# A fused Fourier mixing and SoLU block: sixteen-row exchange of the reciprocals through DRAM, and its two turns at other places

## The chip, the cores and the metric

The kernel runs on one core of one Trainium2 chip. A core has TensorE (PE, with a separate path PEld that loads weights), VectorE (DVE), ScalarE (ACT), GpSimd (POOL) and SyncE (SP), and 16 DMA engines that move data between DRAM and the on-chip memory. Transfers are issued from the instruction queues of SP, ACT and POOL; an issue waits in its queue like any other instruction. The metric is the device time of one execution in microseconds (us), lower is better, as the median of several runs.

## The reference

The first block is a Fourier mixing along the sequence, the second a feed-forward layer whose activation is `h * softmax(h)` followed by a normalization over the 1024 hidden features:

```python
# x: (8, 3136, 256); filt: (1569, 256); w_in: (256, 1024); w_out: (1024, 256)
X = np.fft.rfft(x, axis=1)
y = np.fft.irfft(X * (filt_r + 1j * filt_i)[None], n=3136, axis=1)
h = y.reshape(25088, 256) @ w_in
e = np.exp(h - h.max(-1, keepdims=True))
solu = h * e / (e.sum(-1, keepdims=True) + 1e-09)
mu = solu.mean(-1, keepdims=True)
var = ((solu - mu) ** 2).mean(-1, keepdims=True)
out = ((solu - mu) / np.sqrt(var + 1e-06) * g_ln) @ w_out
```

All data are float32.

## The kernel before

**Work and stages.** The transform of each of the 8 batch elements is done as small matrix products with tables (lines 244 to 424), with passes through DRAM between its parts. Element 0 is transformed ahead of the main loop (up to about 75 us); those of elements 1 to 7 are spread over the main loop, by the steps that `PLAN` gives (line 39), and the last ends at about 1200 us.

The MLP works on 196 blocks of 128 tokens. Two blocks are a pair (98 pairs); both of its matrix products are done on pairs with seven products in place of eight, whose sums and differences POOL makes (`pair_sums`, L782, and `project_sums`, L921). Four blocks are a group g (49 groups). The main loop (L1225) calls `step(k)` for k = 0 to 204; each step writes out by hand what each engine gets and in which order (`manual_schedule`), so that the order of calls in `step` is the order in every queue. A step takes some 6 to 8 us.

**One group on its way.** For block k: PE makes h (`product`, L793, seven products a pair); ACT copies a part out of PSUM (`keep`, L811) and DVE adds the rest and takes the running minimum for the softmax (`finish`, L813: L822 and L825). A `finish` frees a PSUM bank which one of PE's next products needs. Two steps later ACT takes the exponential (L835), DVE multiplies (`normalize`, L847) and a step after that turns the 32x32 squares of the result (`turn`, L865, called the solu turn here). SP then regroups the turned data by eight transfers a pair (`regroup`, L882) into `solu_t`, where hidden features are on partitions; these wait until earlier products have read the buffer. POOL sums them, PE projects them with `w_out` (`project`, L937), ACT scales a part by the reciprocal of the standard deviation (`keep_out`, L968), DVE scales and adds the rest (`finish_out`, L972), and SP stores the output (`store_out`, L980).

**The reciprocals' exchange.** A group's reciprocals come to lie with tokens in an order that differs from the order of the output's rows: POOL computes them for the 128 partitions and four blocks in `deviations` (L890 to L893, by a power of -0.5, into columns 0 to 3 of the 128x32 tile `lines`) in step k = 4g + 6. Then

- in step 4g + 7, after all else that DVE does in that step, `regroup_deviations` (L909) turns `lines` by 32x32 squares on DVE (the first turn, L912), and SP copies rows 0 to 3 of each of the four squares to rows a, a + 32, a + 64 and a + 96 of `corners`, by four transfers of 4 rows of 128 bytes (L914);
- in step 4g + 8, after all else that DVE does, `place_deviations` (L916) turns that half of `corners` on DVE (the second turn, L919). From then on column 2 * (p % 2) + i holds the scale of the i-th output block of pair p.

The first users are `keep_out(p, 0, (0, 0))` on ACT and `finish_out(p, 0, 0, (0, 0), 1)` on DVE in step 4g + 9, for p = 2g. PE's product 6 of that step writes on in the bank that this `keep_out` reads. The 49th group does without the exchange (`product_deviations`, L901).

**What sets the order.** SP's queue holds, in step order: the store of an output pair, the loads of x (four transfers, L270, in some steps), the four transfers of the exchange, eight transfers of `solu_t`, and so on. Every issue waits in order. The framework gives each transfer one of eight completion semaphores in turn, so that an issue also waits for the transfer eight places before it.

Of the kernel before, what the change touches and what calls it, by code (L numbers as in the profile page):

```python
# [9 lines left out]
FP32 = mybir.dt.float32  # L10
# [3 lines left out]
ALU = mybir.AluOpType  # L14
# [4 lines left out]
P = 128  # L19
# [89 lines left out]
def kernel(  # L109
# [10 lines left out]
    nc = tc.nc  # L120
# [12 lines left out]
        name="turn_tbl").ap()  # L133
    one_dram = nc.inline_tensor(np.eye(P, dtype=np.float32), name="one_tbl").ap()

    def pool(name, bufs, space=None, stack=ctx):
        kw = {} if space is None else {"space": space}
        return stack.enter_context(tc.tile_pool(name=name, bufs=bufs, **kw))

    consts = pool("consts", 1)  # L140
    dram = pool("dram", 1, DRAM)
# [2 lines left out]

    d1 = [dram.tile([NS, P, C], FP32, name=f"d1_{e}") for e in range(B)]
    d2 = [dram.tile([NS, P, C], FP32, name=f"d2_{e}") for e in range(B)]
    f_dram = dram.tile([NP, 2, NQ, 2, C], FP32, name="f_dram")

    wf_t = consts.tile([NR, NK], FP32, name="wf_t")
# [9 lines left out]
    neg_half, floor_sb = small_consts[:, 0:4], small_consts[:, 4:5]  # L159
# [278 lines left out]
    with ExitStack() as st:  # L438
# [145 lines left out]
        for i0, n, rows in ((0, 4, P), (4, 4, P), (8, NP - 9, P), (NP - 1, 1, NQ)):  # L584
            f, at = filters[i0]
            nc.sync.dma_start(
                out=f_dram[i0:i0 + n].rearrange("i u q k c -> (u q) i (k c)")[0:rows],
                in_=f[0:rows, at:at + n].rearrange("p i k c -> p i (k c)"))
# [8 lines left out]
        for i in range(pieces):  # L597
# [6 lines left out]
            for j in range(0, 2, size):  # L604
                (nc.scalar.copy, nc.vector.tensor_copy)[j](
                    out=pairs_x[:, 2 * i + j:2 * i + j + size].rearrange("p a c t -> p a t c"),
                               in_=ps[:, j:j + size].rearrange("p a (t c) -> p a t c", t=2))
# [36 lines left out]
        for at, i in enumerate(order):  # L644
# [9 lines left out]
            i0, n = sp.units[i]  # L654
# [42 lines left out]
    lines = small.tile([P, 32], FP32, name="lines", tag="lines", bufs=1)  # L697
    corners = spread.tile([P, 2, 32], FP32, name="corners", tag="corners")
# [59 lines left out]
    def load_de(sp, u, dma=nc.scalar.dma_start):  # L758
# [6 lines left out]
    turns, variances, solu_ts, solu_sums, spreads, rss, pos, ots, places, regrouped = (  # L765
        {} for _ in range(10))
# [93 lines left out]
    def turn(k):  # L860

        g, i = divmod(k, 4)
        if i == 0:
            turns[g] = turn_pools[1 - g % 2].tile([P, DFF // 32, 4, 32], FP32, name=f"turn_{g}", tag="turn")
        nc.vector.transpose(out=turns[g][:, :, i, :],  # L865
                            in_=solus[k].rearrange("p (f j) -> p f j", j=32))
# [23 lines left out]
    def deviations(g):  # L890
        rs = small.tile([P, 4], FP32, name=f"rs_{g}", tag="rs", bufs=2)
        nc.gpsimd.tensor_tensor(out=rs, in0=variances.pop(g), in1=floors.pop(g), op=ALU.add)
        nc.gpsimd.tensor_tensor(out=lines[:, 0:4], in0=rs, in1=neg_half, op=ALU.pow)  # L893

        if 2 * g == pairs - 2:
            spreads[g] = wide = pools["diff"].tile([P, 4, 32], FP32, name=f"wide_{g}", tag="diff")
            nc.gpsimd.tensor_tensor(
                out=wide, in0=turn_t[:, 0:32].rearrange("p (o i) -> p o i", o=1).broadcast_to([P, 4, 32]),
                in1=lines[:, 0:4].rearrange("p (b o) -> p b o", o=1).broadcast_to([P, 4, 32]), op=ALU.mult)

    def product_deviations(g, ps):  # L901

        wide = spreads.pop(g)
        nc.tensor.matmul(out=ps, lhsT=wide.rearrange("p b i -> p (b i)"), rhs=turn_t[:, 32:36],
                         start=True, stop=True)
        rss[g] = corners[:, g % 2, 0:4]
        nc.scalar.copy(out=rss[g], in_=ps)

    def regroup_deviations(g):  # L909

        places = corners[:, g % 2, :]
        nc.vector.transpose(out=lines, in_=lines)  # L912
        for a in range(4):
            nc.sync.dma_start(out=places[a:P:32, :], in_=lines[32 * a:32 * a + 4, :])  # L914

    def place_deviations(g):  # L916

        rss[g] = places = corners[:, g % 2, :]
        nc.vector.transpose(out=places, in_=places)  # L919

    def project_sums(p, step):  # L921
# [44 lines left out]
    def keep_out(p, i, to):  # L966
        rs = out_half(p, i, 0)[1]
        nc.scalar.activation(out=out_half(p, *to)[0], in_=pos[p, 0], func=AFT.Copy, scale=rs)  # L968
# [14 lines left out]
    blocks = NT * B // 2  # L983
# [85 lines left out]
    def step(k):  # L1069
        j, odd = divmod(k, 2)  # L1070
        p = j - (LAG - 1) // 2 if odd else j - (LAG + 1) // 2
        if not 0 <= p < pairs:
            p = None
# [24 lines left out]
        if not odd:  # L1098
# [50 lines left out]
            if 0 <= j - 3 < pairs and j % 2:  # L1149
                deviations((j - 3) // 2)  # L1150
# [13 lines left out]
        else:  # L1164
# [3 lines left out]
                finish(j, k, 1, (k - 1, 1), 2)  # L1168
            for job in early[k]:
                job()  # L1170
            if proj:
                project(p, 1)
                keep_out(p, 0, (0, 0))
                project(p, 2)
                finish_out(p, 0, 0, (0, 0), 1)
# [9 lines left out]
                job()  # L1185
            if 3 <= k < blocks + 3:
                turn(k - 3)
            if hid:
                finish(j, k - 1, 1, None, 0)
                finish(j, k, 0, (k, 0), 2)  # L1190
# [5 lines left out]
                square(k - 3)  # L1196
            for job in first_parts[k]:
                job()
        if k >= 7 and k % 4 == 3 and k - 3 < blocks:
            regroup_deviations((k - 7) // 4)  # L1200
        if k >= 8 and k % 4 == 0 and k - 4 < blocks:
            place_deviations((k - 8) // 4)
        if k < 3:
            convert_w_out(k + 1)
        if k == 2:
# [4 lines left out]
            prepare_w_out(k)  # L1210
        for job in late[k] + loads[k]:
            job()
        if k < 4:
            scale_w_out(k)

# [41 lines left out]
```

## Time and profile before

| what | value |
|---|---|
| time, median of 3 runs | 1580.31 us (1578.24 to 1582.49) |
| time of the profiled execution | 1574.98 us |
| its span, first to last instruction | 1573.1 us |
| granted TensorE clock, mean | 0.996 |
| DVE / ACT / POOL busy share | 80% / 58% / 72% |
| first turn L912 | 48 times, 196 to 209 ns |
| second turn L919 | 48 times, 194 to 214 ns |
| exchange transfers L914 | 192 issues, 0.497 to 1.25 us each on SP, median 0.566 |
| POOL's power L893 | 49 times, 1.02 to 1.37 us |
| mean DMA rate, 160 to 1200 us / 1200 to 1530 us | 211 / 115 GB/s |

The profile is a record of one execution. A line of the timeline gives start and duration in us, the engine, the source line, the operation with the tiles that it writes and reads, how many were merged, and in brackets the engine's idle time before it with what ended it. A line of the waits gives who waited for what, the total in us, how often, and the longest wait. A line of the windows gives the length and then each engine's busy time in the order PE, PEld, DVE, ACT, POOL, the granted clock, the busy share of the DMA engines and the GB/s. The profiled execution was 5.33 us shorter than the median of the runs, so that times of the trace are compared with each other and differences are carried over.

### The profile page before, as it was taken

The page shows a single profiled execution, that of the slowest core. Times are in us where ns is not written, and L with a number is a line of the kernel's source. Part 1 is how long each engine was busy: PE and PEld are TensorE (multiplying, and loading weights), DVE is VectorE, ACT ScalarE, POOL GpSimd, SP SyncE. Part 2 cuts the span into 40 slices and gives each one's busy share as a digit, 9 for nine tenths or more (in the row PEclk, how much of TensorE's full clock was granted, in tenths as well). Part 3 has the DMA queues.
Part 4 walks back from the last instruction along what each step waited for, and adds up shares of the span by engine and source line. Part 5 has one row for each costly group of instructions (what it writes and reads, how often), then busy time and mean ns, then how long its engine had stood idle before and what let it go on. Part 6 is the DMA issues. An engine that isn't in the chain of part 4 may idle for free. (4 is left out here: it accounts for less than half of the span.)

```text
span 1573.1 us, 36938 instructions
## 1 busy us (share of the span) xinstructions
PE 1523.8 (97%) x12748; PEld 1050.9 (67%) x12748; DVE 1254.2 (80%) x2329; ACT 918.6 (58%) x1850; POOL 1135.9 (72%) x1300
## 2 busy tenths in 40 slices
PE   8987999999999999999999999999999999999997
PEld 5633666667666776667666676667766777777776
DVE  5879878897888798977988788877898777777773
ACT  3564655656556656665556656566565665666663
POOL 2577787787768677887768767786766766666675
PEclk9999999999999999999999999999999999999999
DMA  9857787777886788666877588766764554344444
GB/s 246 257 198 211 215 234 219 228 204 206 234 243 199 192 232 249 195 181 185 240 218 197 157 224 234 225 175 181 224 212 124 133 133 122 101 106 116 107 109 115
DMA packets 343795, 298.20 MB, mean 190 GB/s; under 512 B 29451, under 2 KB 313109, under 8 KB 343609
## 3 DMA queue, kind: packets, MB, share of 16 engines
q1 hardware_dynamic: 280408, 175.92, 42.1%
q0 software_dynamic: 29568, 87.33, 18.3%
q10 hardware_dynamic: 33634, 32.58, 7.1%
q8 instruction: 104, 1.70, 0.5%
q14 instruction: 81, 0.66, 0.1%
HBM read 118.02 MB, written 74.84 MB: 123 GB/s over the span
## 5 line engine op out<-in xcount | busy, mean ns | idle before, releaser
L952 PEld LDWEIGHTS o<-w_out_sb,solu_t 128*128 128x128 f32 x3136 | 382.0, 192 | 47.5 <-issue 43.3
L801 PE MATMUL m<-w_in_sb,s 128*128 128x512 f32 x784 | 395.3, 605 | 10.8 <-ACT h L811 5.8
L952 PE MATMUL o<-w_out_sb,solu_t 128*128 128x128 f32 x3136 | 401.0, 276 | 1.8 <-DVE ot L972 1.7
L952 PEld LDWEIGHTS o<-w_out_sb,u 128*128 128x128 f32 x2352 | 306.9, 192 | 141.3 <-issue 107.4
L801 PE MATMUL m<-w_in_sb,y 128*128 128x512 f32 x588 | 307.6, 606 | 10.9 <-DVE nmax L825 8.7
L952 PE MATMUL o<-w_out_sb,u 128*128 128x128 f32 x2352 | 310.4, 275 | 5.2 <-ACT ot L968 3.1
L811 ACT COPY h<-m 128x512 f32<-128x512 f32 x294 | 172.9, 588 | 227.4 <-PE m L801 186.9
L780 POOL TENSOR_TENSOR u<-solu_t 128x512 f32<-128x512 f32 x98 | 138.7, 1415 | 230.7 <-DMA solu_t<-turn 177.1
L847 DVE SCALAR_TENSOR_TENSOR h<-e,h 128x1024 f32<-128x1024 f32 x196 | 296.5, 1513 | 0.4 <-ACT e L835 0.4
L968 ACT ACTIVATE ot<-o,corners 128x128 f32<-128x128 f32 x392 | 143.4, 367 | 254.8 <-PE o L952 240.1
L825 DVE CUSTOM_DVE_ANT_0 h<-m,h 128x512 f32<-128x512 f32 x196 | 134.3, 685 | 162.1 <-ACT h L811 96.6
L855 ACT ACTIVATE h<-h,nmu 128x1024 f32<-128x1024 f32 x196 | 225.0, 1148 | 57.3 <-DVE turn L865 57.2
L865 DVE STREAM_TRANSPOSE turn<-h 128x1024 f32<-128x1024 f32 x196 | 242.3, 1236 | 1.9
L835 ACT ACTIVATE e<-h,nmax 128x1024 f32<-128x1024 f32 x196 | 225.3, 1150 | 4.1 <-DVE h L847 3.4
L780 POOL TENSOR_TENSOR u<-solu_t,u 128x512 f32<-128x512 f32 x98 | 139.5, 1424 | 78.2 <-PE o L952 78.0
L801 PEld LDWEIGHTS m<-w_in_sb,s 128*128 128x128 f32 x784 | 128.0, 191 | 97.3 <-issue 85.0
L780 POOL TENSOR_TENSOR u<-u,solu_t 128x512 f32<-128x512 f32 x98 | 165.7, 1691 | 11.0 <-DMA out_dram<-ot 2.4
L972 DVE SCALAR_TENSOR_TENSOR ot<-o,corners,ot 128x128 f32<-128x128 f32 x299 | 103.5, 347 | 85.4 <-ACT ot L968 53.2
L801 PEld LDWEIGHTS m<-w_in_sb,y 128*128 128x128 f32 x588 | 95.6, 190 | 109.0 <-DVE nmax L825 41.5
L780 POOL TENSOR_TENSOR solu_t<-solu_t,solu_t 128x512 f32<-128x512 f32 x98 | 144.8, 1478 | 0.9
L780 POOL TENSOR_TENSOR s<-y 128x128 f32<-128x128 f32 x196 | 103.0, 526 | 5.2 <-ACT y L423 4.7
L396 PEld LDWEIGHTS py<-wb_t,t 50*64 50x64 f32 x3584 | 57.6, 134 | 42.9 <-issue 20.2
(122 smaller groups left out, 1913.2 us busy)
## 6 DMA issues: line engine op xcount, KB each, us to landing
solu_t<-turn SPq DMA_DIRECT2D x780, 128.0 KB
out_dram<-ot SPq DMA_DIRECT2D x196, 128.0 KB
t<-d POOLq DMA_DIRECT2D x112, 200.0 KB, 6.1
d<-x POOLq DMA_DIRECT2D x100, 200.0 KB, 4.9
t<-d ACTq DMA_DIRECT2D x37, 512.0 KB
f<-f_dram POOLq DMA_DIRECT2D x37, 512.0 KB, 7.5
d<-g POOLq DMA_DIRECT2D x36, 512.0 KB, 4.5
x<-in_x_dram SPq DMA_DIRECT2D x112, 98.0 KB
```

The lines of the kernel that those rows point to most:

```text
L396: nc.tensor.matmul(out=views[g][64 * h:64 * h + 64, cb, i, :], lhsT=t4[rows, i, c0:c0 + 64], rhs=wb_t[rows, 0:N1], start=True, stop=True)
L780: nc.gpsimd.tensor_tensor(out=out, in0=in0, in1=in1, op=op)
L801: nc.tensor.matmul(out=ms[j, bank], lhsT=lhsT, rhs=w_in_sb[:, w, :], start=m in (1, 2, 7), stop=True, skip_group_check=True)
L811: nc.scalar.copy(out=h_half(k, i), in_=ms[j, 0])
L825: nc.vector.tensor_tensor_reduce(out=h_half(k, i), in0=ms[j, bank], in1=h_half(*kept), scale=1.0, scalar=sofar, op0=ALU.add, op1=ALU.min, ...
L835: nc.scalar.activation(out=e, in_=hs[k], func=AFT.Exp, bias=nmaxs.pop(k)[:, 1:2], scale=-1.0, accum_out=esums[g][:, i:i + 1])
L847: nc.vector.scalar_tensor_tensor(out=solu, in0=e, scalar=SHRINK, in1=solu, op0=ALU.mult, op1=ALU.mult, accum_out=nmu)
L855: nc.scalar.activation(out=solu, in_=solu, func=AFT.Square, bias=nmu, scale=-float(DFF), accum_out=variances[g][:, i:i + 1])
L865: nc.vector.transpose(out=turns[g][:, :, i, :], in_=solus[k].rearrange("p (f j) -> p f j", j=32))
L952: nc.tensor.matmul(out=pos[p, bank], lhsT=lhs[:, f, :], rhs=w[:, f, :], start=f == 0 and (m in (1, 2, 7) or alone), stop=True, skip_group_ ...
L968: nc.scalar.activation(out=out_half(p, *to)[0], in_=pos[p, 0], func=AFT.Copy, scale=rs)
L972: nc.vector.scalar_tensor_tensor(out=ot, in0=pos[p, bank], scalar=rs, in1=out_half(p, *kept)[0], op0=ALU.mult, op1=ALU.add)
```

## The change

The first turn of a group follows the solu turn of the same step (4g + 7). One transfer stores the sixteen rows that matter to a tile in DRAM, `exchange`, of which there are two; a second one, issued after the loads of that step, fetches them back in the other order. The second turn stands half a step later: in step 4g + 9, behind the step's first `finish` and the early jobs, ahead of the first projection. So that one access pattern covers the sixteen rows, the reciprocals are in every eighth column (0, 8, 16 and 24) of `lines` and, after the second turn, of `corners`.

```diff
+    exchange = [dram.tile([16, 32], FP32, name=f"exchange_{n}") for n in range(2)]
...
     def deviations(g):
...
-        nc.gpsimd.tensor_tensor(out=lines[:, 0:4], in0=rs, in1=neg_half, op=ALU.pow)
+        nc.gpsimd.tensor_tensor(out=lines[:, 0:32:8], in0=rs, in1=neg_half, op=ALU.pow)
...
     def regroup_deviations(g):
 
+        nc.vector.transpose(out=lines, in_=lines)
+        nc.sync.dma_start(out=exchange[g % 2], in_=lines[0:P:8, :])
+
+    def fetch_deviations(g):
+
+        nc.sync.dma_start(out=corners[0:P:8, g % 2, :],
+                          in_=exchange[g % 2].rearrange("(a b) c -> b a c", b=4))
+
+    def place_deviations(g):
+
         places = corners[:, g % 2, :]
-        nc.vector.transpose(out=lines, in_=lines)
-        for a in range(4):
-            nc.sync.dma_start(out=places[a:P:32, :], in_=lines[32 * a:32 * a + 4, :])
-
-    def place_deviations(g):
-
-        rss[g] = places = corners[:, g % 2, :]
+        rss[g] = places[:, 0:32:8]
         nc.vector.transpose(out=places, in_=places)
...
     def step(k):
...
         else:
             if hid and k >= LAG:
                 product(j, 5)
                 keep(j, k - 1, 1)
                 finish(j, k, 1, (k - 1, 1), 2)
             for job in early[k]:
                 job()
+            if k >= 9 and k % 4 == 1 and k - 5 < blocks:
+                place_deviations((k - 9) // 4)
             if proj:
                 project(p, 1)
                 keep_out(p, 0, (0, 0))
...
             if 3 <= k < blocks + 3:
                 turn(k - 3)
+            if k >= 7 and k % 4 == 3 and k - 3 < blocks:
+                regroup_deviations((k - 7) // 4)
             if hid:
                 finish(j, k - 1, 1, None, 0)
                 finish(j, k, 0, (k, 0), 2)
...
-        if k >= 7 and k % 4 == 3 and k - 3 < blocks:
-            regroup_deviations((k - 7) // 4)
-        if k >= 8 and k % 4 == 0 and k - 4 < blocks:
-            place_deviations((k - 8) // 4)
...
         for job in late[k] + loads[k]:
             job()
+        if k >= 7 and k % 4 == 3 and k - 3 < blocks:
+            fetch_deviations((k - 7) // 4)
```

`product_deviations` takes its columns by the same step of eight. The changed kernel's lines stand one or more further down: the first turn is still L912, the store is L913, the fetch L917, the second turn L924, `keep_out` L973, `finish_out` L977.

## The prediction

> **What bounds the kernel now.** I read, in this order, the page's busy times, the sums by window, the list of waits, and the timeline around the exchange.
>
> ```profile
> PE 1523.8 (97%) x12748; PEld 1050.9 (67%) x12748; DVE 1254.2 (80%) x2329; ACT 918.6 (58%) x1850; POOL 1135.9 (72%) x1300
> ```
> ```profile
> 160.00:1200.00 1040.00, 1024.48 (x9337) 701.17 (x9334) 872.47 (x1603) 621.44 (x1255) 793.55 (x919) 1.00 0.75 211
> 1200.00:1530.00 330.00, 329.69 (x2337) 238.93 (x2336) 243.68 (x486) 203.84 (x412) 225.01 (x247) 1.00 0.44 115
> ```
>
> The first engine column of the windows is PE. While spectra and MLP run together (160 to 1200 us) PE is idle 1040.00 - 1024.48 = 15.5 us; in the tail (1200 to 1530) 0.3 us. So PE sets the time, at a granted clock of 1.00, and nothing that the change touches can win more than those 15.5 us and what the start and the last 45 us hold. The question is how much of the 15.5 us hangs on the exchange.
>
> ```profile
> DVE corners L919 <- DMA corners<-lines: 19.2, 13, 4.1
> ```
> ```profile
> SPq L914 <- DVE lines L912: 133.4, 36, 7.8
> ```
>
> DVE's second turn (L919) waits for the exchange's transfers 13 times, 19.2 us in all, and SP stands 133.4 us in front of the first of them. What a wait of L919 does is seen in group g = 9 (four blocks of tokens; 48 groups use the exchange):
>
> ```profile
> 434.78 5.07 SPq L270 DMA_DIRECT2D x<-in_x_dram  x4
> 439.94 3.91 SPq L914 DMA_DIRECT2D corners<-lines  x4
> ...
> 447.64 0.21 DVE L919 STREAM_TRANSPOSE corners<-corners 128x32 f32<-128x32 f32 x1 [4.08 <-DMA corners<-lines]
> ...
> 448.82 0.68 DVE L825 CUSTOM_DVE_ANT_0 h<-m,h 128x512 f32<-128x512 f32 x1
> ...
> 449.56 1.13 PE L801 MATMUL m<-w_in_sb,y 128*128 128x512 f32 x2 [1.35 <-DVE nmax L825]
> ```
>
> The bracket is the engine's idle time and what ended it. DVE stands 4.08 us at L919; behind it is the next step's `finish` (L825), which frees the bank of product 4; PE stands 1.35 us for that.
>
> **The change, part by part.** Sums are made against the profiled execution, 1574.98 us (span 1573.1 and 1.9 around it). The median of the runs is 1580.31, 5.33 above; I carry the difference over to it.
>
> *Place waits that go.* L919 waits 1 us or more at 187.69 (3.34), 447.64 (4.08), 511.07 (1.00), 637.47 (1.41), 820.64 (1.20), 971.82 (2.31), 1003.73 (1.24), 1035.15 (3.56) and 1061.61 us (1.67). PE idles for `nmax` right behind five of them: at 189.28 (0.34), 449.56 (1.35), 639.00 (0.62), 973.38 (0.84) and 1036.71 (1.14). The gap at 822.30 (1.65) is released by ACT, which had been held by its own DMA issues, and isn't counted. Sum 4.29. In the changed kernel L919 stands behind that `finish`, so even a wait there no longer holds it: **-4.3 us**.
>
> *First turn earlier.* Today L912 follows `normalize`; now it follows the solu turn (L865), 2.4 to 3.9 us earlier in the groups after the first. It needs POOL's power (L893): its end lies at least 0.85 us before the end of that L865 in all 48 groups, so DVE doesn't wait. But its 0.20 us (L912: 48 times, 196 to 209 ns) now stands ahead of L822 and L825, for which PE waits:
>
> ```profile
> 242.06 1.13 PE L801 MATMUL m<-w_in_sb,y 128*128 128x512 f32 x2 [0.62 <-DVE h L822]
> ```
> ```profile
> 1203.29 1.12 PE L801 MATMUL m<-w_in_sb,y 128*128 128x512 f32 x2 [0.32 <-DVE h L822]
> ```
>
> From the end of L822 to PE's next product 1 it is 0.07 us where PE waits (these two), 0.11 to 0.15 in groups 8, 19, 20, 21 and 31, 0.32 or more elsewhere and 1.04 in the tail. So 2 x 0.20 + 5 x 0.13 = **+1.0 us** (ends 0 and 9.6 = 48 x 0.20). Behind `normalize` the same 0.20 goes; no PE gap of the trace ends on the turn that gains it.
>
> *Second turn later.* L919 (0.20 us) leaves the end of the even step and stands in the odd step behind `finish` and ahead of the first `finish_out`. ACT's `keep_out` (L968) needs it. In the quiet group at 722 us `finish` ends at 723.49 and `keep_out` starts at 723.07; so it slips to about 723.75, ends at 724.1, and PE's product 6, which needs it, comes at 725.48. Hidden with 1.4 us to spare; ACT then idles 2.01 us before its next `keep_out`, so its exponential catches up. Cost 0.
>
> *Two legs in place of four transfers.* SP issues two instead of four: 2 x 0.57 us less per group (L914 median 0.566), on an engine that waits 133 us here: 0. But the fetch waits until the store has landed, and behind it on SP stand the eight solu_t transfers (L882) of the next pair, then its two stores of the output. The x loads of the same step lie between the two legs only in the first group. No transfer of 2 KB through DRAM is in the trace. Nearest rows: the present 512-byte transfers, whose packets alone have 128 bytes. In the quiet tail their packets move 1.21 us after the issue and a waiting DVE starts 0.5 to 1.2 us after the last packet (I take 0.65); with queues full the packets come 2 to 5.2 us after the issue. The far end is the 128 KB store of the output, issued at 1542.39 and waited for until 1546.69: 4.3 us. I take the present transfers, for size and queue. Quiet (group 40): L865 ends 1359.07, store issued 1359.50, landed 1361.5, fetch landed 1363.4; L919 is due at about 1369. Full (group 9, where SP is late from L270, so the store still goes at 439.94): 439.94 + 3.58 + 0.65 = 444.17; fetch 444.27 + 3.58 + 0.65 = 448.50. Product 6 without its stall would start at 450.52 - 1.30, and needs the place turn and `keep_out` 0.65 before: 448.57. Just in time. Done so for groups 1 to 46, the fetch misses that point in five (1, 5, 15, 28 and 29, by 0.38, 0.16, 0.84, 0.72 and 1.48: 3.6 us). That is the upper end; the lower is 0, since SP has issued nothing since the store and the fetch finds its own queue empty. I take **+0.5**.
>
> *solu_t.* By the same working its transfers start 0.2 to 3.0 us earlier in 34 of 46 groups, up to 2.0 later in 12. POOL's sums of them end 2.3 us or more before PE reads them in all pairs up to the last three, so this moves PE neither way before the end.
>
> *The end.* There the order on SP does count:
>
> ```profile
> 1535.92 5.66 SPq L882 DMA_DIRECT2D solu_t<-turn  x8
> 1541.68 1.30 SPq L980 DMA_DIRECT2D out_dram<-ot  x2
> ```
> ```profile
> 1546.69 0.37 ACT L968 ACTIVATE ot<-o,corners 128x128 f32<-128x128 f32 x1 [1.78 <-DMA out_dram<-ot]
> ```
> ```profile
> 1547.21 1.13 PE L952 MATMUL o<-w_out_sb,u 128*128 128x128 f32 x8 [1.72 <-ACT ot L968]
> ```
>
> L882 stood directly behind the four corners transfers. Now the store would go at 1531.35 (L865 ends 1530.92), land at 1533.3, and SP is free at about 1533.9, so the store goes 1.9 us earlier and PE's 1.72 us gap can close. But the last pairs' solu_t start at 1543.78, behind a DVE turn that doesn't move, and the gap of 2.02 at 1556.15 waits for sums of them. Between 0 and -1.7 I take **-0.9**.
>
> Sum: -4.3 + 1.0 + 0.5 - 0.9 = -3.7: 1571.3 in the profile's terms, **1576.6** in the runs'.
>
> **The rivals.**
>
> *Given back.* L919 waits 1.0, 1.24 and 1.67 us at 511, 1004 and 1062 us and no PE gap follows: waits are absorbed, and a PE that runs ahead may meet the next late thing. Against it: the gaps after 1204 us are nil, so what is won before is kept. Time 1580.
>
> *More is won.* x loads stand behind solu_t on SP; where it starts earlier, DVE's differences (803.12: idle 1.17 for x, then PE 0.63 at 805.26) and POOL's sums (PE 1.03 at 208.47, and 1.09 at 204.53) could come in time: 2.75 more, with the end's other 0.8 and no late fetch (0.5): -7.7, 1572.6. Against it: in the groups there (2 and 20) solu_t moves by 0.2 and 0.5 us only.
>
> *Slower: DRAM legs late under load.* The point that decides is product 6 of the odd step. With my upper row latencies the slack is -1.48, -0.84, -0.72, -0.38, -0.16, 0.08, 0.26, 0.74 and 0.80 us in the nine tightest. If the two legs together take 1 us more than that, nine groups miss by 10.7 in all: -4.3 + 1.0 + 10.7 - 0.9 = +6.5, 1587. For it: the DMA share is 0.75 in that stretch, and one group's first packet came 5.2 us after its issue. Against it: the emptied queue. The Trainium skill (DMA: Bandwidth & Descriptors, Latency and other measured facts) gives access to HBM, which is the DRAM here, 0.2 us on average and 2 us at high load, and its Specifications add a read-modify-write under 512 B, against rows of 128 B here. No run here shows either yet; if both legs paid 2 us, an estimate by the same slacks is some 38 us slower.
>
> *It doesn't do what it says.* DVE's and SP's listed orders show both turns moved and four transfers made two in each of the 48 groups; PE, ACT and POOL keep their order. Excluded.
>
> **How the numbers follow.** Forecast 0.45 (its own range 1573 to 1580), given back 0.12, more won 0.20, slower 0.23. 0.3% is 4.7 us, about what a measurement of this kernel can tell from no change. Faster than 1575.6: more won, and 0.14 of the forecast: 0.34. Slower than 1585: 0.23. Within: 0.43. The range reaches from 1570 (more won, less 2 us of spread between runs) to 1587, where half of the slower case is left out.
>
> **What would show it.** Right: L919's waits nearly gone, or without a PE gap behind them; the PE gaps at 449 and 1036 us closed; the two gaps behind L822 about 0.2 longer; fetch issued some 2 us after the store in the tail; PE idle between 160 and 1200 us near 12. Wrong: L968 waiting for L919 and PE for L968 in the full groups; SP standing 4 us or more between the legs; POOL waiting longer for solu_t with PE behind it.

## The result, and the profile after

The changed kernel takes 1595.02 us (median of 4 runs, 1591.98 to 1601.16), the kernel before 1579.28 in the same comparison: ratio **1.0104, 95% interval 1.0063 to 1.0144**, slower by some 16 us. The prediction was 1576.6 (1570 to 1587): wrong in sign, and outside the range.

The profiled execution took 1591.98 us (span 1589.9, 16.8 more than before, granted clock 0.992). The busy times, and the windows with the same columns as before:

```profile
PE 1533.9 (96%) x12748; PEld 1054.8 (66%) x12748; DVE 1260.2 (79%) x2329; ACT 919.2 (58%) x1850; POOL 1125.4 (71%) x1300
```
```profile
160.00:1200.00 1040.00, 1016.56 (x9248) 694.12 (x9240) 864.43 (x1578) 611.97 (x1237) 771.84 (x909) 1.00 0.75 208
1200.00:1530.00 330.00, 330.00 (x2348) 237.89 (x2347) 249.14 (x493) 204.84 (x413) 227.43 (x251) 1.00 0.45 117
```

PE idles 23.4 us between 160 and 1200 us (15.5 before) and not at all in the tail. It is also 10.1 us *busier* with as many instructions. Its clock explains some 6.8 of them: it is at 0.50 for 13.7 us more than before, 3.4 of these ahead of 160 us and 10.2 behind (below). The rest isn't explained. I set the start of PE's product 1 of each pair against the same one of before. It is 2.9 us later already at pair 0, ahead of the first exchange; 3.3 at pair 10; 10.6 at pair 15; 13.6 at pair 23 and 13.5 at pair 55; 18.3 at pair 57; 17.3 at pair 61; from pair 72 to the end 16.6 to 17.1. So the time is lost in a few places of the stretch with spectra, and the tail is neutral. The steps at pairs 15, 23 and 57 (5.7, 4.0 and 3.6 us) make 13.2 of the 14.2 us lost between pair 0 and the end; PE's stalls at 331, 463 and 991 us, which are shown below, lie there. The waits of the changed kernel (who, for what, total us, times, longest):

```profile
ACT ot L973 <- DVE corners L924: 42.0, 33, 5.2
...
DVE corners L924 <- DMA corners<-exchange: 16.6, 8, 5.4
DVE diff L280 <- DMA x<-in_x_dram: 15.9, 11, 3.6
...
PE o L957 <- ACT ot L973: 13.3, 8, 4.8
```

The last line is new in size (3.1 before, all of it behind 1530 us): PE waits for `keep_out`, `keep_out` for the second turn, the second turn for the fetch. ACT's 42.0 us alone are no loss: they are as long where no transfer is late (the turns alone, below). DVE's wait for x is 9.4 us before. What PE waits for between 160 and 1200 us, after and before:

```profile
PE o L957 <- ACT ot L973: 11.4, 6, 4.8
PE m L802 <- DVE nmax L826: 5.4, 4, 2.2
```
```profile
PE m L801 <- DVE nmax L825: 6.0, 7, 1.4
PE m L801 <- ACT h L811: 3.7, 3, 1.9
```

There is no wait for `keep_out` in that stretch before. SP's own waits between 160 and 1200 us, first after, then the line of before that answers to it:

```profile
SPq L917 <- DMA exchange<-lines: 146.9, 33, 6.7
...
SPq L883 <- DMA t<-d: 41.6, 14, 7.9
```
```profile
SPq L914 <- DVE lines L912: 76.9, 22, 7.8
```

SP stands 4.5 us on average between store and fetch in each of these 33 groups; in the kernel before it stood for the first turn, in 22 groups and for half as long in all. Group g = 9, the same as in the prediction, over all engines:

```profile
442.04 1.74 SPq L985 DMA_DIRECT2D out_dram<-ot  x2
442.57 0.17 DVE L912 STREAM_TRANSPOSE lines<-lines 128x32 f32<-128x32 f32 x1
...
443.89 2.30 SPq L271 DMA_DIRECT2D x<-in_x_dram  x4
...
446.52 0.53 SPq L913 DMA_DIRECT2D exchange<-lines  x1
...
454.61 0.69 DVE L280 TENSOR_TENSOR diff<-x 113x512 f32<-113x512 f32 x1 [1.58 <-DMA x<-in_x_dram]
454.80 0.57 SPq L917 DMA_DIRECT2D corners<-exchange  x1
455.46 8.33 SPq L883 DMA_DIRECT2D solu_t<-turn  x8
...
456.87 1.02 PE L802 MATMUL m<-w_in_sb,y 128*128 128x512 f32 x2
...
461.90 0.21 DVE L924 STREAM_TRANSPOSE corners<-corners 128x32 f32<-128x32 f32 x1 [5.38 <-DMA corners<-exchange]
462.20 0.37 ACT L973 ACTIVATE ot<-o,corners 128x128 f32<-128x128 f32 x1 [6.41 <-DMA solu_t<-turn]
...
462.71 2.05 PE L957 MATMUL o<-w_out_sb,u 128*128 128x128 f32 x8 [4.82 <-ACT ot L973]
```

The first turn is done at 442.74, but SP is still issuing output stores and x loads, so the store goes 3.8 us later. Its 128-byte packets move for 11 to 13 ns each, the last of them 7.7 us after the issue. The fetch is issued 8.3 us behind the store, its packets come 4.0 to 6.1 us later. From turn to turn it is 19.2 us, and PE stands 4.82. The bracket of `keep_out` names solu_t, but what it needs and what ended 0.1 us before it is the second turn.

PE's clock, in two stretches of the same group (the granted clock is the third number from the end):

```profile
457.90:462.10 4.20, 0.00 (x0) 0.00 (x0) 0.20 (x1) 0.00 (x0) 4.11 (x8) 1.00 1.05 297
462.10:465.50 3.40, 2.79 (x13) 2.82 (x14) 2.88 (x6) 1.86 (x4) 0.62 (x2) 0.50 1.03 249
```

Behind the stall PE runs at half clock for 3.4 us. The same follows the stalls that end at 331.25 us (2.02, with 1.60 just before) and 991.02 us (2.88). Between 160 and 1530 us the kernel before has no such stretch. Each costs about 1.7 us, 5 in all, and shows up as busy time, not as idle time.

### The profile page after: what moved, and what is told of

The parts are those of the page before. It is cut to its first block, busy times and chain, and to the rows that moved or that the text cites. A ratio compares the mean times of both kernels' runs of the same rounds, so it can differ in the third digit from the quotient of the medians.

```text
span 1589.9 us, 36711 instructions
## 1 busy us (share of the span) xinstructions
PE 1533.9 (96%) x12748; PEld 1054.8 (66%) x12748; DVE 1260.2 (79%) x2329; ACT 919.2 (58%) x1850; POOL 1125.4 (71%) x1300
## 4 chain that ended last, share of the span: by engine, by line
PE 78%; DMA 11%; DVE 4%; issue 2%; SPq 2%; POOL 1%; ACT 1%; ACTq 0%; DVEq 0%; POOLq 0%
PE o L957 33%; PE m L802 32%; DMA solu_t<-turn 4%; PE py L397 4%; PE pc L327 3%; PE pb L327 2%; PE pa L295 2%; DMA x<-in_x_dram 2%; DMA t<-d 2%; DMA exchange<-lines 1%; SPq L883 1%; PE pa L252 1%; PE py L420 1%; DMA out_dram<-ot 1%; DMA corners<-exchange 1%
## 5 line engine op out<-in xcount | busy, mean ns | idle before, releaser
L957 PE MATMUL o<-w_out_sb,u 128*128 128x128 f32 x2352 | 312.6, 277 | 16.1 <-ACT ot L973 13.3
L848 DVE SCALAR_TENSOR_TENSOR h<-e,h 128x1024 f32<-128x1024 f32 x196 | 301.1, 1536 | 0.4 <-ACT e L836 0.4
L973 ACT ACTIVATE ot<-o,corners 128x128 f32<-128x128 f32 x392 | 143.2, 367 | 267.6 <-PE o L957 193.9
L977 DVE SCALAR_TENSOR_TENSOR ot<-o,corners,ot 128x128 f32<-128x128 f32 x299 | 103.6, 347 | 90.3 <-ACT ot L973 63.7
L781 POOL TENSOR_TENSOR solu_t<-solu_t,solu_t 128x512 f32<-128x512 f32 x98 | 159.5, 1627 | 0.9
L781 POOL TENSOR_TENSOR u<-u,solu_t 128x512 f32<-128x512 f32 x98 | 147.6, 1506 | 11.0 <-DMA out_dram<-ot 2.0
L781 POOL TENSOR_TENSOR s<-y 128x128 f32<-128x128 f32 x196 | 99.4, 507 | 7.0 <-DMA x<-in_x_dram 6.6
```

What stands on the lines that cost most here:

```text
L781: nc.gpsimd.tensor_tensor(out=out, in0=in0, in1=in1, op=op)
L848: nc.vector.scalar_tensor_tensor(out=solu, in0=e, scalar=SHRINK, in1=solu, op0=ALU.mult, op1=ALU.mult, accum_out=nmu)
L957: nc.tensor.matmul(out=pos[p, bank], lhsT=lhs[:, f, :], rhs=w[:, f, :], start=f == 0 and (m in (1, 2, 7) or alone), stop=True, skip_group_ ...
L977: nc.vector.scalar_tensor_tensor(out=ot, in0=pos[p, bank], scalar=rs, in1=out_half(p, *kept)[0], op0=ALU.mult, op1=ALU.add)
```

## The experiments

Three theories were put against each other: **late turn** (called "legs" or "second turn late" below: two transfers through DRAM, one after the other, land too late for the second turn), **turns** (the new places of the turns themselves cost), and **SP** ("SP's own time": in the stretch with spectra SP is nearly full, and each issue and each stand there delays the x loads, solu_t and stores behind it). All ratios are against the kernel before on the same chip. The last two columns are from SP's waits between 160 and 1200 us: what it waits for PE, DVE, ACT or POOL, which have yet to make data or to read a buffer (the time that it has to spare), and what it waits for transfers.

| kernel | ratio (95%) | spare | for transfers |
|---|---|---|---|
| before | 1 | 240 | 120 |
| the change | 1.0104 (1.0063 to 1.0144) | 137 | 273 |
| turns moved alone | 0.9992 (0.9970 to 1.0015) | 199 | 165 |
| legs alone, old turns | 1.0152 (1.0119 to 1.0185) | 211 | 218 |
| stale fetch | 0.9922 (0.9900 to 0.9944) | 268 | 131 |
| turns moved, idle legs | 1.0263 (1.0234 to 1.0292) | 95 | 287 |
| two of four transfers | 0.9938 (0.9913 to 0.9963) | 262 | 130 |
| both legs on ACT | 1.0052 (1.0032 to 1.0073) | 253 | 200 |
| four transfers on ACT | 1.0350 (1.0318 to 1.0383) | 226 | 251 |
| fetch later | 1.0032 (1.0009 to 1.0055) | 283 | 143 |
| fetch unread | 1.0065 (1.0039 to 1.0091) | 133 | 273 |
| x loads behind the store | 1.0013 (0.9997 to 1.0028) | 200 | 210 |
| x loads and stores behind | 0.9989 (0.9972 to 1.0006) | 281 | 117 |
| product, first pair short | 0.9956 (0.9940 to 0.9972) | 318 | 126 |
| product on PE | 0.9958 (0.9937 to 0.9978) | 328 | 121 |
| product, 34 groups | 0.9946 (0.9925 to 0.9967) | 323 | 126 |

Times are medians; the last two columns and all waits are of one profiled execution each, which for fetch later, fetch unread and x loads behind the store was 5 to 8 us above the median, for the idle legs 9.5 below.

**The turns alone.** The kernel before, with both turns moved.

```diff
             if 3 <= k < blocks + 3:
                 turn(k - 3)
+            if k >= 7 and k % 4 == 3 and k - 3 < blocks:
+                regroup_deviations((k - 7) // 4)
...
+            if k >= 9 and k % 4 == 1 and k - 5 < blocks:
+                place_deviations((k - 9) // 4)
             if proj:
                 project(p, 1)
...
-        if k >= 7 and k % 4 == 3 and k - 3 < blocks:
-            regroup_deviations((k - 7) // 4)
-        if k >= 8 and k % 4 == 0 and k - 4 < blocks:
-            place_deviations((k - 8) // 4)
```

> The kernel before with both turns moved to their new places, and the exchange left as it was: four transfers from SBUF to SBUF, issued by SP behind the first turn. Theory 'legs' (the loss is that two transfers through DRAM, one after the other, land too late for the second turn, so that ACT's keep_out and with it PE wait): the turns cost nothing and their gain is kept, 1573 to 1579 us, no PE gap of 2 us or more behind keep_out. Rival 'turns' (the second turn half a step later and the first turn ahead of finish are what costs): as the changed kernel, 1590 to 1600 us. Rival 'SP' (SP standing between the two legs holds up what is queued behind it): as theory 'legs', since nothing stands here.

Measured 1578.4 us beside 1581.5 for the kernel before. Theory "turns" falls. The gaps that the prediction wanted closed are closed, but PE idles 15.6 us between 160 and 1200 us, as before (15.5): others have opened. One of them, first on PE, then on ACT:

```profile
383.92 1.10 PE L801 MATMUL m<-w_in_sb,s 128*128 128x512 f32 x2 [1.69 <-ACT h L811]
```
```profile
382.07 0.38 ACTq L316 DMA_DIRECT2D t<-d  x1
382.49 0.66 ACTq L761 DMA_DIRECT2D de<-de_tbl  x1
383.19 0.58 ACT L811 COPY h<-m 128x512 f32<-128x512 f32 x1 [4.76 <-PE o L952]
```

ACT had stood in front of a load that it issues itself; its copy, for which PE waits, is queued behind. What held that issue the trace doesn't name. The second turn at its new place makes ACT wait, but PE only behind 1530 us:

```profile
ACT ot L968 <- DVE corners L919: 42.7, 41, 1.9
...
PE o L952 <- ACT ot L968: 1.4, 2, 0.9
```

**The legs alone.** The changed kernel with `regroup_deviations` and `place_deviations` called where the kernel before calls them.

> The changed kernel with both turns put back to the places of the kernel before (first turn behind normalize, second turn at the end of step 4g + 8), and the exchange through DRAM kept. Theory 'legs': in the trace of the changed kernel store and fetch together take some 5 to 6 us in the quiet tail and 6 to 14 us in the full groups, against 3 to 7 us between the two turns in the kernel before, so DVE waits at the second turn ahead of finish in most groups: 1620 to 1670 us. Rival 'turns': back to the kernel before, 1575 to 1585 us. Rival 'SP': SP stands as in the changed kernel, 1590 to 1600 us.

1602.31 us: less than "legs" asked for, more than either rival. DVE waits 41.1 us at the second turn (15 times) and PE 32.7 for nmax behind it; SP stands 117.7 us between the legs over the whole run (189.1 in the change). Late landing at the old places costs some 8 us more than at the new ones, though the intervals overlap: the move seems to pay for part of what the legs cost.

**The stale fetch.**

```diff
-                          in_=exchange[g % 2].rearrange("(a b) c -> b a c", b=4))
+                          in_=exchange[max(g - 1, 0) % 2].rearrange("(a b) c -> b a c", b=4))
```

> The changed kernel, with the fetch reading the DRAM tile that the group before has written, so it need not wait for its own group's store; the scale of each group's output is that of the group before, so this part of the computation is not that of the reference. Takes away the wait for the store's landing (48 times, 189 us on SP), leaves every instruction and transfer. Theory 'legs': the second turn is no longer late but in one or two groups, 1573 to 1581 us. Rival 'turns': 1590 to 1600 us. Rival 'SP': 1573 to 1581 us as well.

1566.29 us, faster than expected and faster than the turns alone by 0.7%, with the same two transfers through DRAM. So neither DRAM nor the turns lose the time; the wait of the fetch does, whether through the late turn or through SP.

**The idle legs.** The moved turns with their four transfers, and the two legs beside them into a tile that nobody reads.

```diff
...
             nc.sync.dma_start(out=places[a:P:32, :], in_=lines[32 * a:32 * a + 4, :])
+        nc.sync.dma_start(out=exchange[g % 2], in_=lines[0:P:8, :])
+
+    def fetch_deviations(g):
+
+        nc.sync.dma_start(out=unused[0:P:8, g % 2, :],
+                          in_=exchange[g % 2].rearrange("(a b) c -> b a c", b=4))
...
```

> As the kernel with only the turns moved (four transfers from SBUF to SBUF that the second turn uses), and besides them the two legs through DRAM at their places in SP's order, into a tile that nobody reads: SP stands between the legs as in the changed kernel, but no turn waits for them. Theory 'legs': 1574 to 1582 us, within 3 us of the kernel with the moved turns alone. Rival 'SP' (what is late are the solu_t transfers, x loads and output stores behind the fetch on SP): 1588 to 1600 us. Rival 'turns': 1590 to 1600 us, like the kernel with the moved turns.

1621.09 us, 2.7% above the turns alone, though no turn waits for the legs; DVE waits 46.0 us for x in place of 12.4. This is where "late turn" as the only cause falls. It is more than "SP" gave. SP has four issues a group more than in the changed kernel here, so the issues themselves may be a second cause. The next ones take the two apart.

**Two of the four transfers,** both turns moved.

```diff
-        for a in range(4):
+        for a in range(0, 4, 2):
...
```

> Both turns moved, and of the four transfers from SBUF to SBUF only two issued; the scales of two of the four tile rows of each group are then missing, so this part of the computation is left out. SP issues as few exchange transfers as in the kernel with the stale fetch (1566.3 us), and nothing goes through DRAM. Theory 'SP's own time' (in the stretch with spectra SP is nearly full; from 160 to 1200 us it waits for DVE, PE or ACT to have data ready, the only time that it has to spare, 240 us in the kernel before, 199 with the turns moved, 137 in the changed kernel, 268 with the stale fetch, 95 with the idle legs; each issue and each stand there delays x loads, solu_t and stores): 1563 to 1572 us. Rival 'second turn late' (only when the turn is late matters): the turns are in time already with four, so 1575 to 1581 us.

1569.38 us. Two small issues a group fewer on SP are worth 0.54% (8.5 us), without DRAM, as much as the stale fetch gained within the intervals. The changed kernel issues as few, so it should have this gain too; the prediction had put it at nothing.

**The legs on ACT.**

```diff
-        nc.sync.dma_start(out=exchange[g % 2], in_=lines[0:P:8, :])
+    def store_deviations(g):
+
+        nc.scalar.dma_start(out=exchange[g % 2], in_=lines[0:P:8, :])
...
-        nc.sync.dma_start(out=corners[0:P:8, g % 2, :],
+        nc.scalar.dma_start(out=corners[0:P:8, g % 2, :],
...
```

> The changed kernel with both legs through DRAM issued by ACT: the store behind square in step 4g + 7, the fetch behind keep_out of step 4g + 8. The two legs and the moved turns stay, SP has no part in them. Theory 'SP's own time': SP has 96 issues and its stand between the legs less, 1555 to 1572 us. Rival 'second turn late': the legs still follow one another and the store goes later, 1590 to 1605 us. A second rival, that ACT now stands at the fetch and its copies for PE come late: 1575 to 1600 us, with PE waiting for ACT's h.

1588.69 us: the second rival. The late turn is gone (0.2 us of waits at it), SP has 253 us to spare, and PE now waits 15.1 us, 15 times, for ACT's h.

**The four transfers on ACT.** As above with the four transfers, turns moved.

> Both turns moved, the four transfers from SBUF to SBUF kept but issued by ACT behind square in step 4g + 7. Theory 'SP's own time': 1555 to 1570 us, since SP has 192 issues less. Rival 'second turn late': no better than with the turns moved alone, 1575 to 1581 us. Rival that four issues of 0.37 us on ACT, with waits for the transfer eight places before, delay ACT's copies as much as they cost SP: 1578 to 1590 us.

1633.55 us, beyond every expectation. ACT stands at the issues:

```profile
ACT g L365 <- DMA corners<-lines: 50.4, 16, 10.0
...
PE pb L326 <- ACT g L365: 19.8, 6, 4.5
```

ACT's copies, for which PE waits, are queued behind, and 47.8 us between 160 and 1530 run at half clock. A stand costs more here on the engine that works for PE at once than on SP.

**The fetch later.** Behind the first four solu_t transfers of step 4g + 8.

```diff
                 regroup(j - 3, 0)
+                if k >= 8 and k % 4 == 0 and k - 4 < blocks:
+                    fetch_deviations((k - 8) // 4)
                 regroup(j - 3, 1)
...
-        if k >= 7 and k % 4 == 3 and k - 3 < blocks:
-            fetch_deviations((k - 7) // 4)
```

> The changed kernel with the fetch moved on SP behind the first four solu_t transfers of step 4g + 8. SP's stand at the fetch (189 us in 48 places) should nearly go, and the fetch is issued and lands some 2 to 5 us later. Theory 'SP's own time': 1572 to 1588 us. Rival 'second turn late': the turn is later still, 1598 to 1630 us, with ACT's keep_out waiting for the second turn in more groups than in the changed kernel (33 times, 42 us).

1585.35 us. SP has its spare time back (283 us; it stands 50.6 us for the store, 146.9 in the change), x is on time (DVE waits 2.3 us for it, 15.9 in the changed kernel), and the turn is later than ever:

```profile
PE o L957 <- ACT ot L973: 18.8, 9, 5.1
```

Three of these stalls are followed by 20.5 us at half clock. Less stand and a later turn give a better time than the change. Beside the two of four transfers, which has as many issues and neither stand nor late turn, it is 0.94% slower: **a late turn with a third of the stand costs some 15 us** (10 to 20 by the intervals).

**The fetch unread.** The reverse: the stand stays, the turn is never late.

```diff
+    unused = spread.tile([P, 2, 32], FP32, name="unused", tag="unused")
...
-        nc.sync.dma_start(out=corners[0:P:8, g % 2, :],
+        nc.sync.dma_start(out=unused[0:P:8, g % 2, :],
```

> The changed kernel, with the fetch writing a tile that nobody reads; the second turn turns a tile of zeros, so the scales of the output are left out. Same issues on SP, same stand between the legs, but the second turn is never late: takes the late turn away and leaves SP's stand. The other half was taken away in the kernel with the fetch behind four solu_t (stand mostly gone, turn late: 1585.4 us), and both in the one with the stale fetch (1566.3 us); the changed kernel has both (1595.0 us). If SP's stand alone costs: 1578 to 1592 us, with PE waiting for nmax or h behind DVE's or POOL's waits for x and solu_t. If it costs only through the late turn: 1565 to 1570 us.

1589.2 us: 1.27% above the two of four transfers, which has as many issues and no stand, and 1.43% above the stale fetch, which has the same two legs. So **SP's stand alone costs some 20 us** (14 to 26 by the intervals). Its waits show a way from SP to PE, here beside those of the stale fetch:

```profile
DVE diff L280 <- DMA x<-in_x_dram: 33.6, 19, 4.3
...
PE m L803 <- DVE nmax L827: 17.4, 16, 2.6
```
```profile
PE m L802 <- DVE nmax L826: 7.1, 5, 2.5
...
DVE diff L280 <- DMA x<-in_x_dram: 6.8, 5, 3.1
```

The x loads are queued behind the fetch and the solu_t transfers behind it; DVE's difference needs x, and the `finish` that frees PE's bank stands behind the difference. The time goes in many small waits here, none of 2 us or more between 160 and 1530 us.

**The x loads behind the store,** and then the output stores too. The calls that load x in step 4g + 6 are made in step 4g + 7 behind `regroup_deviations`; in the second kernel `store_out` of step 4g + 6 as well.

```diff
...
+            if k % 4 == 3 and proj and p - 1 >= 0 and p - 1 not in last and p - 1 in ots:
+                store_out(p - 1)
+            if k % 4 == 3:
+                for job in rows[k - 1]:
+                    job()
             if hid:
                 finish(j, k - 1, 1, None, 0)
...
```

> The changed kernel with the x loads of step 4g + 6 moved on SP behind the exchange's store of step 4g + 7 (half a step later). Theory 'the store queues behind what SP issued just before it' (group 9: four x loads issued 443.89 to 446.19 us, store issued 446.52, landed only 8.3 us later): in the groups with x loads the store is issued up to 3 us earlier, lands 3 to 6 us earlier, and both SP's stand and the late turn shrink: 1568 to 1588 us. Rival: the latency is that of small transfers through DRAM, whatever stands ahead: legs unchanged, 1590 to 1600 us. Rival: the x loads themselves are then late, 1595 to 1615 us, with DVE waiting for x.

> As the kernel with the x loads behind the exchange's store, and the two output stores of step 4g + 6 moved behind it too. Theory 'the store queues behind what SP issued just before it': in the tail, where the changed kernel has 2.8 to 5.7 us between the issues of the two legs and only the output stores are ahead, it falls to about 1.8 us (the one group of the tail with nothing ahead has 1.80); time 1565 to 1588 us. Rival 'small DRAM transfers are slow': the tail keeps 2.8 us or more. Rival: SP now stands at the first turn ahead of output stores and x loads, and gives back what is won: 1588 to 1605 us.

1583.08 and 1578.58 us beside 1579.65: the first gets back most of the loss, the second all, with two DRAM legs a group as in the change. SP's stand falls from 146.9 to 94.7 and 17.0 us, and no turn is late in the second. It is still 0.7% above the stale fetch; DVE waits 16.1 us for x, in place of 6.8. What moved is seen in the quiet tail. SP there in the changed kernel and with all behind the store:

```profile
1373.75 1.30 SPq L985 DMA_DIRECT2D out_dram<-ot  x2
1375.82 0.55 SPq L913 DMA_DIRECT2D exchange<-lines  x1
1378.83 0.56 SPq L917 DMA_DIRECT2D corners<-exchange  x1
```
```profile
1361.93 0.54 SPq L913 DMA_DIRECT2D exchange<-lines  x1
1362.56 1.21 SPq L985 DMA_DIRECT2D out_dram<-ot  x2
1363.87 0.57 SPq L917 DMA_DIRECT2D corners<-exchange  x1
```

From issue to issue of the legs it is 3.38 us in the median of 13 groups of the tail (1.80 to 5.67) where the output stores go ahead, and 1.96 where they go behind; but these 1.96 are mostly the time in which SP issues the output stores. The packets tell more. From the issue of the store to its last packet it is 2.80 us in the tail (median) and 4.51 where spectra run; with all behind the store 1.34 and 2.54. In the first case the packets of 128 bytes move among and behind the last of 1024 bytes from the output stores. The Trainium skill (DMA: Bandwidth & Descriptors, Queues, rings and completion order) says that each of the 16 engines consumes the transfers of one issuing queue in order; these rows fit that. They don't show that the queue is what counts. With both legs on ACT, where the output stores are on SP's queue and issued 2.2 us or more before, the store still takes 2.45 us in the tail. A queue without output stores doesn't spare it here.

Nor is the whole round trip shorter in the median. The fetch now goes behind output stores and x loads: 3.91 us to its last packet where spectra run, in place of 1.79. From the end of the first turn to the last packet of the fetch it is 8.8 us in the median of 33 groups, and 8.9 in the change; only the longest falls, from 18.2 to 12.7. What the order seems to win is that SP has other transfers to issue between the legs, and that the longest round trips are cut.

**The exchange as a product on PE,** for all groups, as the last group does it: no turns, no transfers.

```diff
-        if 2 * g == pairs - 2:
-            spreads[g] = wide = pools["diff"].tile([P, 4, 32], FP32, name=f"wide_{g}", tag="diff")
+        spreads[g] = wide = spread.tile([P, 4, 32], FP32, name=f"wide_{g}", tag="wide")
...
-            if k == blocks + 4:
-                product_deviations(pairs // 2 - 1, places[p])
+            if k >= 12 and k % 4 == 0 and k <= blocks + 4:
+                product_deviations((k - 8) // 4, places[p])
...
```

> The kernel before with the exchange of every group made as that of its last group: a product on PE with a tile of the reciprocals spread by POOL, a copy of four columns by ACT, no turns and no transfers. Theory 'SP's own time': SP has 192 issues less than before and nothing to stand at, as good as the kernel with two of four transfers (1569.4 us) or better, less what PE pays: 0.1 to 0.4 us a group by the one such product in the trace (two matmuls, 0.42 us with their weight loads), 5 to 19 us. Together 1560 to 1582 us. Rival: PE's share decides, 1585 us or more. Rival: POOL (0.41 us for the spread tile, 20 us in all) makes the sums of solu_t late: PE waits for POOL's u, 1585 us or more.

1573.47 us. In this kernel the first group's product starts a sum in a PSUM bank where the first pair's own sum is still running, so a part of that pair is left out. The next has a tile of its own for it, and the one after it uses the product for the first 34 groups only:

```diff
+            if k == 9:
+                product_deviations(0, psum("places_0")[:, 0, 0:4])
```

> The exchange of every group by a product on PE, as in the run before, but with the first group's product in a PSUM tile of its own. 1570 to 1577 us by that run (1573.5). If SP's own time is what the changed kernel lost, this kernel, which has no exchange on SP, keeps its gain with the whole computation done. If it was gained only because part of the first pair was left out, 1578 us or more.

> The product on PE for the first 34 groups alone (the stretch with spectra); the 14 groups of the tail use the kernel before's turns and four transfers. In the tail PE has no gap (0.3 us in 330) and SP's transfers of the exchange cost it nothing, so the product's price there is pure loss: 14 groups at 0.1 to 0.4 us. Theory 'SP's own time counts in the stretch with spectra only': 1.4 to 5.6 us faster than the product everywhere, 1565 to 1574 us. Rival, that the tail too gains by having no transfers: as the product everywhere or slower.

1572.62 and 1571.51 us beside 1578.95, with the whole computation done: **0.42% (0.22 to 0.63) and 0.54% (0.33 to 0.75) faster than before**, and some 1.5% faster than the change. Windows of the product for all groups:

```profile
160.00:1200.00 1040.00, 1032.00 (x9431) 711.77 (x9430) 872.45 (x1546) 630.67 (x1294) 816.90 (x956) 1.00 0.76 211
1200.00:1530.00 330.00, 330.00 (x2351) 240.40 (x2351) 237.37 (x457) 204.63 (x422) 230.60 (x259) 1.00 0.43 114
```

PE idles 8.0 us in the stretch with spectra in place of 15.5. In the tail it pays: its lead over the kernel before shrinks from 5.75 us at pair 72 to 3.02 at pair 97, 2.73 us in 12.5 groups, 0.22 a group; with the product for 34 groups the lead stays (3.02 and 3.17). The difference between the two times is too small for their intervals.

## Why the prediction was wrong, point by point

By the ratios, in us of 1580, one step after the other: turns moved, -1.3 (interval -4.7 to +2.4); two issues fewer on SP, -8.5; SP's stand alone, +20; the late turn on top of it, +6 (the change against the fetch unread; their intervals overlap). Sum +16. The order of the steps decides this split: a late turn with a third of the stand costs +15, the stand alone +20, and both together only +26. So the two don't add up; either alone loses most of the time. In the change's own trace the late turn is where it is lost: PE waits 11.4 us for `keep_out` between 160 and 1200 us (none before) and runs 10.2 us at half clock behind these waits, some 16.5 in all, while its waits for `nmax` are no longer than before (5.4 and 6.0). Both ways have one root, the wait of the fetch for the store: with that wait gone and all else kept (the stale fetch), the kernel is 0.8% faster than before.

- *Place waits that go* (-4.3) and *first turn earlier* (+1.0): the waits went, the gaps at 449 and 1036 us too, and with the turns alone PE waits 0.09 us longer behind L822 in each of the two places that were named, in place of 0.2. The sum of -3.3 is inside the interval of the turns alone, but so is nothing: other gaps opened, as the rival *given back* had it.
- ***Two legs in place of four transfers* is the step that failed:** "on an engine that waits 133 us here: 0". The 133.4 us were a sum over all groups. Only 77 of it lie where spectra run, in 22 groups; group 9, where SP comes 3.8 us late to the exchange, has none. Spare time of a quiet group can't be spent in a full one. Both of the term's parts were off: issues fewer gain 8.5, the stand of the fetch, which the text named with what is queued behind it and gave no price, costs 20 by itself. What it did price, the latency of the legs, is the next point.
- *Late fetch* (+0.5, from 0 to 3.6), of the same paragraph: mis-sized, some 16.5 in the change's trace. The reason given for the low end, "the fetch finds its own queue empty", was about the wrong leg: the fetch took 1.79 us to its last packet in the median where spectra run, well under the 3.58 that was worked with for a full group, but the store 4.51 (2.3 to 7.7). Moved ahead by 2.4 us or more, the store now goes right behind the output stores and x loads. In the tail it is 3.4 us from issue to issue of the legs in place of 2.0; in group 9 it is 8.3 where 4.3 was worked out, and from the fetch to the turn 7.1 in place of 4.2. The half clock behind long stalls wasn't in the price at all.
- *solu_t* "moves PE neither way": by that working SP is free sooner; it was later. In the change's own trace PE still hardly waits for POOL (1.9 us between 160 and 1200, 1.6 before), but with the fetch unread it waits 4.1.
- *The end*: -0.3 from pair 97 to the last instruction, for -0.9 (between 0 and -1.7).
- *Slower: DRAM legs late under load* had the right side and the right place (PE at product 6, ACT at `keep_out`), at 1587. Two of the signs that the prediction named for being wrong came: PE waits for `keep_out` in full groups, and SP stands 4.5 us between the legs. ACT's wait for the second turn is no such sign, as the turns alone show. The rival was priced by the late turn alone, and by latencies that were still too short. The price that the Trainium skill gives for small accesses (DMA: Bandwidth & Descriptors, Latency and other measured facts), put beside it as an estimate of +38, isn't borne out as a cost of DRAM itself: with the stale fetch, two DRAM transfers cost no more than two between SBUF tiles (0.9922 and 0.9938).
- *More is won*: of its gaps, the one at 204.53 us is ended by DVE's `nmax` (1.08 us), not by POOL's sums.

What stays open: which wait holds an ACT-issued load, as at 382 us; why the late turn and the stand cost less together than apart (that PE, when it stalls for one, gives the other time to catch up, is likely but not shown); and what a single transfer of all sixteen rows from SBUF to SBUF would do, which was not tried.

## What to carry to other kernels

A queue's idle time is worth something only where the queue is idle: look at its waits in the stretch and the groups in which the change adds a wait, not at their sum. A small transfer lands late while large ones issued just before it are still moving (2.80 us in the tail behind the output stores, 1.34 ahead of them), on another queue too (2.45); so its place in time among them set its latency here more than that it went through DRAM. A dependent round trip puts what its queue can't fill of its latency on that queue; before paying that, see whether there is other work to issue between the legs, or whether an engine that is idle there (or a short product) can do the exchange.

## What the runs showed of the hardware that was not expected

- PE stalls are often followed by 3.4, 6.8 or 10.2 us at clock 0.50. In the sixteen profiles there are 39 stalls of 2 us or more between 160 and 1530 us. The ten of 3.65 us or more all have such a stretch, which begins in the stall or within 3.4 us of its end (4.82 us in the changed kernel by 3.4, 5.11 in the fetch-later kernel by 6.8). Of the 29 shorter ones 17 have it, down to 2.02 us (331.25 us in the changed kernel, 1.60 just before), and 12 have not, up to 3.64 us (455.64 us with the legs alone). Five stretches have no stall of 2 us near them. The Trainium skill (TensorE: Matmul & The Clock Gate, Part 1: The HAM clock gate) gives an idle window of about 3.4 us, which runs on its own, before the clock is halved. The lengths of the stretches agree; but a stall of 2.02 us can't fill such a window, so that an idle window isn't all that counts here. What else does, these runs don't show.
- A round trip's first leg through DRAM, 16 rows of 128 bytes, takes 1.80 us from issue to the next issue where most of the output stores ahead have moved (1218.71 to 1220.51 us in the changed kernel), and 8.28 us in group 9; the packets themselves take 11 to 13 ns in both.
- The start differs between executions, ahead of the first exchange: a stretch of 6.8 us at half clock lies at 52.5 us in the changed kernel and at 33.5 us with the stale fetch, and none there in the kernel before. That fits the 2.9 us at pair 0, so that these are likely no part of the change.
